# Attention transposes of two tiles packed four to a PSUM bank, output sums copied whole and moved by DMA, two sums inverted at once, another order of steps

## The chip, the cores and the metric

The kernel runs on one core of a Trainium2 chip. The metric is the device time of one execution in microseconds (us). A profile shows one execution: its span from the first to the last instruction, and the work of the engines TensorE (PE, with its weight loads as PEld), VectorE (DVE), ScalarE (ACT), GpSimd (POOL) and SyncE (SP, which here only issues DMAs).

## The reference, cut to what matters

```python
def _attn_ref(q, k, v, proj):            # q, k, v: 2 x 8 x 768 x 64; proj: 64 x 6
    q_bits = (np.einsum('bhsd,dk->bhsk', q, proj) > 0).astype(np.int64)
    k_bits = (np.einsum('bhsd,dk->bhsk', k, proj) > 0).astype(np.int64)
    q_bucket, k_bucket = np.sum(q_bits * powers, -1), np.sum(k_bits * powers, -1)
    mask = q_bucket[:, :, :, None] == k_bucket[:, :, None, :]
    scores = np.where(mask, scale * np.matmul(q, k.transpose(0, 1, 3, 2)), -1000000000.0)
    attn = np.exp(scores - np.max(scores, axis=-1, keepdims=True))
    attn = attn / (np.sum(attn, axis=-1, keepdims=True) + 1e-09)
    return np.matmul(attn, v)

def reference(**kwargs):
    x = _attn_ref(...)                   # -> 1536 tokens x 512
    x = _moe_ref(x, ...)                 # 8 experts, all on every token, weights from 8 rounds of row/column scaling
    return _moe2_ref(x, ...)             # 8 experts, each on 192 tokens, assigned greedily by logit
```

## The kernel before, in words

The program has three stages: attention (the first 267 us of the trace), the first mixture of experts and the second. The change touches attention alone.

Attention works in 8 **passes** of two heads each (`n` = 0 to 7). A pass has 12 **tiles** of 128 queries, six of each head; `t` counts tiles over all passes, `r` = 0 to 11 within a pass. Two neighbouring tiles make a **unit** (`unit`, line 267), whose output is 256 queries by 64 columns. Matmuls use float32r, a number split into a high and a low part where it needs more digits. A tile goes through these functions:

- `qk` (line 273): scores into one of two PSUM tiles `S0`, `S1`; four matmuls, the bucket mask is part of the operands.
- `soft` (282): the negated row maximum, on DVE. `expo` (287): exp and row sum, on ACT, into `e`. `inv` (293): 1/(sum + 1e-9), two DVE instructions on one column. `norm` (298): `e` times it, on POOL, into another tile `a`.
- `tr` (304): six 128x128 transposes of `a` on PE, three into each of two PSUM tiles `tp` (three buffers, which the preparation below also uses). `trh` (314): the high part, copied by ACT to `ah`. `trl` (318): the low part, on DVE to `al`.
- `av` (324): V times the transposed tiles of a unit, 12 matmuls of 256 columns into one half of the PSUM tile `O`, six in each of two steps. The stationary operand holds the high part of V beside the low part, so the two halves of `O`'s 128 partitions must still be added.
- `xa` (334): two ACT copies of 64 partitions by 256 columns carry them to `xm` and `xc`, one of them to other partitions. `xp` (348), on POOL and for the second head only: add the two, split the sum into high and low part for the next stage (`X`).

Beside that, `ahead` (362) prepares the next pass in its tiles r = 0 to 9: transposes of q and k (r = 0 to 3), bucket bits (4, 5), mask rows (6 to 9). `stack` (157) then moves q, k and mask rows into the operand tiles by DMA, six DMAs of 192 KB each after r = 1 and after r = 3, two after r = 7 and r = 9. `ahead_v` (367) prepares V on POOL and, in r = 11, issues the loads of q, k and v of the pass after next.

The order of all engines' instructions in attention is written out by hand: a loop over steps `t` (line 399) calls the functions in the order of `PLAN` or one of `PLANS` (lines 26 to 40), each with a lag, so that ('tr0', 3) in step t works on tile t - 3. Each engine runs its instructions in that order. SP issues its DMAs in that order too, and the weights of the next stage (`wgr`, line 462, and `raw`, line 432) stand behind the last of them in its queue.

Of the kernel before, what the change touches and what calls it, by code (L numbers as in the profile page):

```python
# [24 lines left out]

PLAN = (('norm', 2), ('qk', 0), ('soft', 0), ('tr0', 3), ('av', 5), ('expo', 1), ('pp', 0), ('th0', 3), ('inv', 1),
        ('tr1', 3), ('xa', 5), ('pa', 0), ('tl0', 3), ('pv', 0), ('pd', 0), ('th1', 3), ('tl1', 3), ('xp', 6))
PLANS = {
# [11 lines left out]
}  # L40
PREP_V = (3, 3, 6, 9)
# [14 lines left out]
def kernel(ctx, tc, q, k, v, proj, wg1, w1, w2, wg2, w1b, w2b, out):  # L56
# [225 lines left out]
    def soft(t):  # L282
        w = ap.tile([128, 4], F32, name="w", bufs=6)
        nc.vector.tensor_reduce(w[:, 0:1], Sp[t % 2], op=OP.max, axis=AX.X, negate=True)  # L284
        EN[t] = w

    def expo(t):
        w = EN[t]
        e = ap.tile([128, S], F32, name="e", bufs=2)
        nc.scalar.activation(e, Sp[t % 2], AF.Exp, bias=w[:, 0:1], scale=1.0, accum_out=w[:, 1:2])  # L290
        EN[t] = (e, w)

    def inv(t):
        e, w = EN[t]
        nc.vector.tensor_scalar(w[:, 2:3], w[:, 1:2], 1e-9, None, op0=OP.add)
        nc.vector.reciprocal(w[:, 3:4], w[:, 2:3])  # L296

    def norm(t):
        e, w = EN[t]
        a = ap.tile([128, S], F32, name="a", bufs=3)  # L300
        nc.gpsimd.tensor_tensor(a, e, w[:, 3:4].to_broadcast([128, S]), op=OP.mult)  # L301
        EN[t] = a

    def tr(t, c):
        u, i = divmod(t, 2)
# [6 lines left out]
        TP[t, c] = p[:, :384].rearrange("p (a b) -> p a b", a=3)  # L312

    def trh(t, c):
        u, i = divmod(t, 2)
        nc.scalar.activation(AT[u][0][:, 3 * c:3 * c + 3, i, :], TP[t, c], AF.Copy)  # L316

    def trl(t, c):
        u, i = divmod(t, 2)
        ah, al = AT[u]  # L320
        nc.vector.tensor_tensor(al[:, 3 * c:3 * c + 3, i, :], TP[t, c], rd(ah[:, 3 * c:3 * c + 3, i, :]), op=OP.subtract)  # L321


    def av(t):
        u, c = divmod(t, 2)
        n, s, j = unit(u)
        o = Op[:, u % 2]
        ah, al = AT[u]
        for kt in range(3 * c, 3 * c + 3):
            for a in (ah, al):  # L330
                nc.tensor.matmul(o, VS[n][:, kt, s].rearrange("p a d -> p (a d)"), a[:, kt].rearrange("p a b -> p (a b)"),  # L331
                                 start=(kt == 0 and a is ah), stop=(kt == R - 1 and a is al))

    def xa(t):
        u, c = divmod(t, 2)
        if c == 0:
            return
# [29 lines left out]
    def ahead_v(t):  # L367
# [829 lines left out]
```

## Time and profile before

| | |
|---|---|
| median of three runs | 1591.05 us (1590.64 to 1592.92) |
| the profiled execution | 1590.74 us, span 1589.0 us |
| PE busy over the span | 1557.7 us (98%) |
| DVE, ACT, POOL busy over the span | 812.7 us (51%), 471.3 us (30%), 269.0 us (17%) |
| busy from 14 to 268 us (254 us of attention): PE, DVE, ACT, POOL | 242.90, 221.51, 224.17, 214.01 us |
| granted TensorE clock there | 0.99 of full speed |

A matmul's recorded duration holds its fill and drain and overlaps the next one, so "busy" of PE says little. The distance from one matmul's start to the next one's start is what it really takes of the engine's time. The table's last two lines show a stage in which four engines are all above 84% busy, which the shares over the whole span hide.

### The profile page before, as it was taken

How to read it: one execution, taken by the hardware profiler on the slowest of the kernel's cores; microseconds unless marked ns; L12 is line 12 of the kernel's file. 1: busy time of each engine (PE TensorE's matmuls, PEld its weight loads, DVE VectorE, ACT ScalarE, POOL GpSimd, SP SyncE). 2: the span in 40 equal slices, each digit the busy share in tenths (PEclk: the TensorE clock that was granted, in tenths of full speed). 3: DMA queues.
4: the chain of work that ended last, by engine and by line, in shares of the span. 5: the costliest groups of instructions: out<-in, count | busy, mean ns of one | idle time of the engine just before them, and what ended most of it. 6: DMA issues, size and time to landing. Idle time of an engine off the chain costs nothing.

```text
span 1589.0 us, 21566 instructions
## 1 busy us (share of the span) xinstructions
PE 1557.7 (98%) x8482; PEld 1307.7 (82%) x8482; DVE 812.7 (51%) x1974; ACT 471.3 (30%) x950; POOL 269.0 (17%) x309
## 2 busy tenths in 40 slices
PE   8999998999999999999999999999999999899998
PEld 6888887788888888888888888888887767888998
DVE  6998888623433324333333332134677377667533
ACT  6998997212211210221221121021121210011343
POOL 4888886020000000000000000000000000111221
PEclk9999999999999999999999999999999999999999
DMA  8665561021200210110120020011000105555531
GB/s 189 150 146 134 124 157 37 31 93 37 70 1 14 71 35 14 53 54 1 40 80 0 14 80 27 1 53 53 1 14 14 41 31 196 174 189 188 191 137 31
DMA packets 81782, 117.75 MB, mean 74 GB/s; under 512 B 42960, under 2 KB 44496, under 8 KB 81680
## 3 DMA queue, kind: packets, MB, share of 16 engines
q1 hardware_dynamic: 75920, 105.15, 22.5%
q0 software_dynamic: 2144, 6.49, 1.3%
q10 hardware_dynamic: 3616, 4.72, 0.8%
q8 instruction: 67, 1.10, 0.3%
q14 instruction: 35, 0.29, 0.1%
HBM read 84.10 MB, written 7.86 MB: 58 GB/s over the span
## 4 chain that ended last, share of the span: by engine, by line
PE 89%; DVE 3%; ACT 3%; DMA 2%; POOL 1%; issue 1%; SPq 1%; ACTq 0%; POOLq 0%; DVEq 0%
PE hp L563 33%; PE yp L582 29%; PE hp L931 5%; PE yp L878 4%; PE tp L311 3%; PE O L331 3%; PE yp L983 3%; PE S L280 3%; PE yp L986 2%; PE sp L1065 1%; PE tp L202 1%; ACT e L290 1%; PE yp L988 1%; ACT ah L316 1%; DVE w L284 1%
## 5 line engine op out<-in xcount | busy, mean ns | idle before, releaser
L563 PE MATMUL hp<-X,big 128*128 128x512 f32 x2304 | 534.2, 392 | 0.0
L563 PEld LDWEIGHTS hp<-X,big 128*128 128x128 f32 x2304 | 431.9, 188 | 94.8
L582 PE MATMUL yp<-big 128*128 128x512 f32 x2016 | 462.2, 390 | 0.0
L582 PEld LDWEIGHTS yp<-big 128*128 128x128 f32 x2016 | 378.2, 188 | 79.5
L564 ACT ACTIVATE big<-hp 128x512 fp32r<-128x512 f32 x176 | 105.3, 598 | 763.0 <-PE hp L563 762.7
L565 DVE SCALAR_TENSOR_TENSOR big<-hp,big 128x512 fp32r<-128x512 f32 x176 | 121.6, 691 | 257.1 <-ACT big L564 257.0
L587 DVE SCALAR_TENSOR_TENSOR acc<-yp,P,acc 128x512 f32<-128x512 f32 x72 | 54.1, 751 | 259.3 <-PE yp L582 259.3
L859 POOL DMA_INDIRECT raw<-x2h,who x2 | 2.1, 1066 | 945.1 <-DVE wg2b L1050 944.8
L301 POOL TENSOR_TENSOR a<-e,w 128x768 f32<-128x768 f32 x96 | 140.7, 1468 | 45.4 <-DVE w L296 26.4
L321 DVE TENSOR_TENSOR al<-tp,ah 128x384 fp32r<-128x384 f32 x192 | 102.8, 547 | 18.9 <-ACT ah L316 18.5
L311 PE MATMUL tp<-ident,a 128*128 128x128 f32 x576 | 94.4, 276 | 8.7 <-ACT hot L233 2.9
L931 PE MATMUL hp<-raw,big 128*128 128x192 f32 x496 | 94.7, 337 | 2.1 <-ACT raw L910 2.1
L316 ACT ACTIVATE ah<-tp 128x384 fp32r<-128x384 f32 x192 | 90.9, 487 | 16.2 <-PE tp L311 15.7
L284 DVE TENSOR_REDUCE w<-S 128x1 f32<-128x768 f32 x96 | 91.1, 949 | 4.8 <-PE S L280 4.8
L311 PEld LDWEIGHTS tp<-ident,a 128*128 128x128 f32 x576 | 67.1, 140 | 25.1 <-issue 5.8
L290 ACT ACTIVATE e<-S,w 128x768 f32<-128x768 f32 x96 | 86.5, 901 | 0.7 <-POOL a L301 0.6
L428 DVE TENSOR_TENSOR big<-raw,big 128x1024 fp32r<-128x1024 f32 x63 | 76.6, 1221 | 14.1 <-ACT big L427 10.7
L931 PEld LDWEIGHTS hp<-raw,big 128*128 128x128 f32 x496 | 80.7, 192 | 3.6 <-ACT raw L910 2.4
L331 PE MATMUL O<-ah,vv 128*128 128x256 f32 x288 | 80.6, 309 | 0.5 <-ACT xm L346 0.5
L427 ACT ACTIVATE big<-raw 128x1024 fp32r<-128x1024 f32 x63 | 64.6, 1053 | 28.0 <-DMA raw<-in_moe_w_dram 25.0
L331 PE MATMUL O<-al,vv 128*128 128x256 f32 x288 | 72.8, 282 | 0.0
L538 DVE SCALAR_TENSOR_TENSOR junk<-acc,wg2b 128x512 bf16<-128x512 f32 x96 | 66.0, 688 | 1.9
(254 smaller groups left out, 1592.3 us busy)
## 6 DMA issues: line engine op xcount, KB each, us to landing
raw<-in_moe_w_dram SPq DMA_DIRECT2D x67, 512.0 KB, 3.3
big<-in_moe_w_dram SPq DMA_DIRECT2D x32, 1024.0 KB, 8.4
qa<-qhi SPq DMA_DIRECT2D x32, 192.0 KB, 3.8
qb<-qlo SPq DMA_DIRECT2D x16, 192.0 KB, 4.5
ka<-khi SPq DMA_DIRECT2D x16, 192.0 KB, 3.6
ka<-klo SPq DMA_DIRECT2D x16, 192.0 KB, 4.0
kb<-khi SPq DMA_DIRECT2D x16, 192.0 KB, 3.6
rv<-in_v_dram SPq DMA_DIRECT2D x16, 192.0 KB, 4.3
```

Of the source, the lines that this page charges most:

```text
L284: nc.vector.tensor_reduce(w[:, 0:1], Sp[t % 2], op=OP.max, axis=AX.X, negate=True)
L290: nc.scalar.activation(e, Sp[t % 2], AF.Exp, bias=w[:, 0:1], scale=1.0, accum_out=w[:, 1:2])
L301: nc.gpsimd.tensor_tensor(a, e, w[:, 3:4].to_broadcast([128, S]), op=OP.mult)
L311: nc.tensor.transpose(p[:, x * 128:x * 128 + 128], EN[t][:, (3 * c + x) * 128:(3 * c + x) * 128 + 128], ident)
L316: nc.scalar.activation(AT[u][0][:, 3 * c:3 * c + 3, i, :], TP[t, c], AF.Copy)
L321: nc.vector.tensor_tensor(al[:, 3 * c:3 * c + 3, i, :], TP[t, c], rd(ah[:, 3 * c:3 * c + 3, i, :]), op=OP.subtract)
L331: nc.tensor.matmul(o, VS[n][:, kt, s].rearrange("p a d -> p (a d)"), a[:, kt].rearrange("p a b -> p (a b)"), start=(kt == 0 and a is ah), ...
L563: nc.tensor.matmul(t, a, b, start=(i == 0), stop=(i == len(prods) - 1))
L564: nc.scalar.activation(hh[:, f], t, AF.Relu)
L565: nc.vector.scalar_tensor_tensor(hl[:, f], t, 0.0, rd(hh[:, f]), op0=OP.max, op1=OP.subtract)
L582: nc.tensor.matmul(t, a, b, start=(i == 0), stop=(i == len(prods) - 1))
L931: nc.tensor.matmul(opened[f], w[:, d, f * 128:f * 128 + 128], xt[:, d], start=(d == 0), stop=(d == HP - 1))
```

## The change

Four things change. **Transposes:** the twelve transposes of a unit's two tiles go into three PSUM places of four each (a place is one whole bank of 512 columns) instead of four places of three; `trh` and `trl` then handle 512 columns at a time, three times in a unit. The second place holds two blocks of the one tile and two of the other, so `ah` and `al` are laid out tile by tile, and `av` reads two stretches of 128 columns for its 256. **Sums:** V's high part now always stands first, so `xa` copies all 128 partitions of the unit's half of `O` in one ACT instruction; what has to change partitions is moved by DMA, one for the first head, two for the second head (from a tile `x1` with one buffer). **Inversion:** `inv` handles the sums of a unit's two tiles at once. **Order:** one plan of two steps (an even and an odd one) instead of five plans; `norm` writes in place, `e` has five buffers, and the lags grow: norm 3, transposes 4 to 6, av 7 and 8, `xa` 8, `xp` 10.

```diff
-PLAN = (('norm', 2), ('qk', 0), ('soft', 0), ('tr0', 3), ('av', 5), ('expo', 1), ('pp', 0), ('th0', 3), ('inv', 1),
...
+PLANS = ((('tr', 6, 2), ('norm', 3), ('qk', 0), ('av', 8, 1), ('tr', 4, 0), ('pv', 0), ('soft', 0), ('expo', 1), ('th', 6, 2),
...
     def inv(t):
         e, w = EN[t]
-        nc.vector.tensor_scalar(w[:, 2:3], w[:, 1:2], 1e-9, None, op0=OP.add)
-        nc.vector.reciprocal(w[:, 3:4], w[:, 2:3])
+        nc.vector.tensor_scalar(w[:, 4:6], w[:, 2:4], 1e-9, None, op0=OP.add)
+        nc.vector.reciprocal(w[:, 6:8], w[:, 4:6])
...
-        nc.gpsimd.tensor_tensor(a, e, w[:, 3:4].to_broadcast([128, S]), op=OP.mult)
+        nc.gpsimd.tensor_tensor(e, e, w[:, i:i + 1].to_broadcast([128, S]), op=OP.mult)
...
-        for x in range(3):
-            nc.tensor.transpose(p[:, x * 128:x * 128 + 128], EN[t][:, (3 * c + x) * 128:(3 * c + x) * 128 + 128], ident)
+        for y in range(4):
+            i, kt = divmod(4 * x + y, R)
+            nc.tensor.transpose(p[:, y * 128:y * 128 + 128], EN[t + i][:, kt * 128:kt * 128 + 128], ident)
...
-        nc.scalar.activation(AT[u][0][:, 3 * c:3 * c + 3, i, :], TP[t, c], AF.Copy)
+        ah = AT[t // 2][0].rearrange("p i a b -> p (i a b)")[:, 512 * x:512 * x + 512]
+        nc.scalar.activation(ah, TP[t, x], AF.Copy)
...
-                nc.tensor.matmul(o, VS[n][:, kt, s].rearrange("p a d -> p (a d)"), a[:, kt].rearrange("p a b -> p (a b)"),
+                nc.tensor.matmul(o, VS[n][:, kt, s].rearrange("p a d -> p (a d)"), a[:, :, kt],
...
     def xa(t):
...
-        nc.scalar.activation(xc[m0:m0 + 64, cs], o[c0:c0 + 64], AF.Copy)
-        nc.scalar.activation(xm[m0:m0 + 64, cs], o[m0:m0 + 64], AF.Copy)
+        if s == 0:
+            xm, xc = XP[n, j] = (ap.tile([128, 256], F32, name="xm", bufs=4), ap.tile([128, 256], F32, name="xc", bufs=4))
+            nc.scalar.activation(xm, o, AF.Copy)
+            nc.sync.dma_start(xc[:D], xm[D:])
+        else:
+            xm, xc = XP[n, j]
+            x1 = ap.tile([128, 256], F32, name="x1", bufs=1)
+            nc.scalar.activation(x1, o, AF.Copy)
+            nc.sync.dma_start(xm[D:], x1[:D])
+            nc.sync.dma_start(xc[D:], x1[D:])
...
-        if r % 2 == 0 and r >= 4 and n + 1 < NP:
-            prep_v(n + 1, r // 2 - 2)
+        if r in (8, 10) and n + 1 < NP:
+            prep_v(n + 1, r // 2 - 4)
+        if r in (0, 2) and 0 < n < NP:
+            prep_v(n, r // 2 + 2)
```

How the instructions stand now is shown at three places. The lines in rows of the changed kernel are those of its own file, some 12 to 15 lower.

On SP, from the mask rows of one pass (`kb<-hot`) over the loads (`rq`, `rk`, `rv`) to the next pass's q stack (`qa`, `qb`), before:

```order
L163 DMA kb_122<-hot_981 64x768 x2
L94 DMA rq<-in_q_dram 128x6x64 x2
L94 DMA rk<-in_k_dram 128x6x64 x2
L94 DMA rv<-in_v_dram 128x6x64 x2
L163 DMA qa_115<-qhi 64x768 x2
L163 DMA qb_117<-qlo 64x768
L163 DMA qa_115<-qhi 64x768 x2
L163 DMA qb_117<-qlo 64x768
```

and the same place in the changed kernel:

```order
L151 DMA kb_122<-hot_896 64x768 x2
L331 DMA xc<-xm 64x256
L82 DMA rq<-in_q_dram 128x6x64 x2
L82 DMA rk<-in_k_dram 128x6x64 x2
L82 DMA rv<-in_v_dram 128x6x64 x2
L331 DMA xc<-xm 64x256
L151 DMA qa_115<-qhi 64x768 x2
L151 DMA qb_117<-qlo 64x768
L151 DMA qa_115<-qhi 64x768 x2
L151 DMA qb_117<-qlo 64x768
L336 DMA xm<-x_1102 64x256
L337 DMA xc<-x_1102 64x256
```

A DMA of a finished sum (`xc<-xm`) has come between the mask rows and the loads, and the two DMAs that empty `x1` stand behind the six of the q stack.

On SP at the end of attention, from the last mask rows (`kb_118`) to the gate weights (`wgr`) and expert weights (`raw`) of the next stage, before:

```order
L163 DMA kb_118<-hot_3401 64x768 x2
L462 DMA wgr<-in_moe_w_gate_dram 128x4x8
L432 DMA raw<-in_moe_w_dram 128x1024 x4
L437 DMA raw<-in_moe_w_dram 128x2x512 x4
```

and in the changed kernel, from the last pass's sums on:

```order
L331 DMA xc<-xm 64x256 x3
L336 DMA xm<-x_3639 64x256
L337 DMA xc<-x_3639 64x256
L336 DMA xm<-x_3676 64x256
L337 DMA xc<-x_3676 64x256
L336 DMA xm<-x_3695 64x256
L337 DMA xc<-x_3695 64x256
L447 DMA wgr<-in_moe_w_gate_dram 128x4x8
L417 DMA raw<-in_moe_w_dram 128x1024 x4
L422 DMA raw<-in_moe_w_dram 128x2x512 x4
```

The weights of the next stage now stand behind the DMAs of the very last sum.

On PE, one step in the middle of attention, before (one tile's transposes in two groups of three, scores, one half of a unit's V product):

```order
L311 MATMUL tp<-ident,a 128x128 x3
L280 MATMUL S0_123<-ka0_120,qa0_119 128x512 [waits Activation_49]
L280 MATMUL S0_123<-ka0_120,qa0_119 128x256
L280 MATMUL S0_123<-kb0_122,qb0_121 128x512
L280 MATMUL S0_123<-kb0_122,qb0_121 128x256
L311 MATMUL tp<-ident,a 128x128 x3
```

and in the changed kernel the end of an odd step, with the first two groups of the even step behind it:

```order
L298 MATMUL tp<-ident,e 128x128 x8
L268 MATMUL S_123<-ka_120,qa_119 128x512
L268 MATMUL S_123<-ka_120,qa_119 128x256
L268 MATMUL S_123<-kb_122,qb_121 128x512
L268 MATMUL S_123<-kb_122,qb_121 128x256
L320 MATMUL O<-ah,vv 128x256
```

An even step has two groups of four transposes and an odd step one; the eight in the first row are the odd step's group and the even step's first. The number of transposes, scores and V products of two steps is the same as before.

## Rows read from the trace of the kernel before

**Rows 1.** Busy time by stretch: start:end, length; each engine busy (instructions); clock, DMA share, GB/s

```profile
80.00:112.00 32.00, 31.18 (x227) 27.96 (x224) 28.66 (x71) 29.21 (x71) 27.66 (x28) 1.00 0.63 136
```

**Rows 2.** PE in order of time, first bit matmul of passes 0 and 6: start, us

```profile
25.12 0.45 PE L202 MATMUL tp<-qhi,pjh 128*128 128x384 f32 x1
...
213.13 0.34 PE L202 MATMUL tp<-qhi,pjh 128*128 128x384 f32 x1
```

**Rows 3.** PE in order of time, one step in the middle of attention

```profile
60.44 0.49 PE L311 MATMUL tp<-ident,a 128*128 128x128 f32 x3
60.68 0.60 PE L280 MATMUL S<-ka,qa 128*128 128x512 f32 x2
...
61.47 0.49 PE L311 MATMUL tp<-ident,a 128*128 128x128 f32 x3
...
62.51 0.34 PE L225 MATMUL tp<-bits,pat 128*128 128x384 f32 x1
```

**Rows 4.** Chain of waits in order of time, one piece: start, us, what

```profile
56.42 1.05 PE tp L202 x6
```

**Rows 5.** Costliest groups of the page: line, engine, tiles, count | busy, mean ns | idle before

```profile
L564 ACT ACTIVATE big<-hp 128x512 fp32r<-128x512 f32 x176 | 105.3, 598 | 763.0 <-PE hp L563 762.7
L565 DVE SCALAR_TENSOR_TENSOR big<-hp,big 128x512 fp32r<-128x512 f32 x176 | 121.6, 691 | 257.1 <-ACT big L564 257.0
...
L321 DVE TENSOR_TENSOR al<-tp,ah 128x384 fp32r<-128x384 f32 x192 | 102.8, 547 | 18.9 <-ACT ah L316 18.5
...
L316 ACT ACTIVATE ah<-tp 128x384 fp32r<-128x384 f32 x192 | 90.9, 487 | 16.2 <-PE tp L311 15.7
```

**Rows 6.** Groups of ACT from 14 to 268 us, same columns

```profile
L345 ACT ACTIVATE xc<-O 64x256 f32<-64x256 f32 x48 | 18.2, 378 | 5.3 <-PE O L331 3.9
```

**Rows 7.** Groups of POOL from 14 to 268 us, same columns

```profile
L301 POOL TENSOR_TENSOR a<-e,w 128x768 f32<-128x768 f32 x96 | 140.7, 1468 | 45.4 <-DVE w L296 26.4 <-ACT hot L233 12.9 <-ACT xm L346 2.4
...
L358 POOL TENSOR_TENSOR xm<-xm,xc 128x256 f32<-128x256 f32 x23 | 16.9, 734 | 0.2 <-ACT xm L346 0.2
...
L359 POOL TENSOR_TENSOR X<-xm,zero 128x256 fp32r<-128x256 f32 x23 | 14.1, 613 | 1.8
```

**Rows 8.** SP in order of time: last mask rows of a pass, then a load

```profile
71.19 1.11 SPq L163 DMA_DIRECT2D kb<-hot  x2
72.35 1.34 SPq L94 DMA_DIRECT2D rq<-in_q_dram  x2
```

**Rows 9.** SP in order of time: first and last DMAs of one q stack

```profile
111.61 1.16 SPq L163 DMA_DIRECT2D qa<-qhi  x2
...
115.65 0.56 SPq L163 DMA_DIRECT2D qb<-qlo  x1
```

**Rows 10.** PE in order of time, first q transposes of a pass and what they waited for

```profile
140.21 0.52 PE L173 MATMUL tp<-ident,rq 128*128 128x128 f32 x3 [0.93 <-DMA rq<-in_q_dram]
```

**Rows 11.** Tile `rq`: from DMA issue to landing

```profile
DMA to landing us min/median/max: 2.3/3.4/4.5
```

**Rows 12.** DMA issues from 226 to 250 us: tiles, count, KB each, median us to landing

```profile
raw<-in_moe_w_dram SPq DMA_DIRECT2D x3, 512.0 KB, 4.5
kb<-hot SPq DMA_DIRECT2D x2, 192.0 KB, 2.8
wgr<-in_moe_w_gate_dram SPq DMA_DIRECT2D x1, 16.0 KB, 2.6
```

**Rows 13.** PE in order of time, from the last units into the next stage

```profile
265.34 0.38 PE L331 MATMUL O<-ah,vv 128*128 128x256 f32 x1 [0.53 <-ACT xm L346]
...
267.14 0.40 PE L476 MATMUL sp<-X,wgs 128*16 128x512 f32 x1
...
276.81 2.35 PE L563 MATMUL hp<-X,big 128*128 128x512 f32 x9
```

**Rows 14.** ACT in order of time: first three weight conversions of the next stage

```profile
268.13 2.96 ACT L427 ACTIVATE big<-raw 128x1024 fp32r<-128x1024 f32 x3
```

**Rows 15.** DVE in order of time: first weight conversion and what it waited for

```profile
270.47 1.22 DVE L428 TENSOR_TENSOR big<-raw,big 128x1024 fp32r<-128x1024 f32 x1 [3.41 <-POOL X L360]
```

More of the change, by code (lines that the diff above doesn't have):

```diff
@@ L282, in soft @@
     def soft(t):
-        w = ap.tile([128, 4], F32, name="w", bufs=6)
-        nc.vector.tensor_reduce(w[:, 0:1], Sp[t % 2], op=OP.max, axis=AX.X, negate=True)
-        EN[t] = w
+        if t % 2 == 0:
+            EN[t] = EN[t + 1] = ap.tile([128, 8], F32, name="w", bufs=5)
+        nc.vector.tensor_reduce(EN[t][:, t % 2:t % 2 + 1], Sp[t % 2], op=OP.max, axis=AX.X, negate=True)
     def expo(t):
-        w = EN[t]
-        e = ap.tile([128, S], F32, name="e", bufs=2)
-        nc.scalar.activation(e, Sp[t % 2], AF.Exp, bias=w[:, 0:1], scale=1.0, accum_out=w[:, 1:2])
+        w, i = EN[t], t % 2
+        e = ap.tile([128, S], F32, name="e", bufs=5)
+        nc.scalar.activation(e, Sp[i], AF.Exp, bias=w[:, i:i + 1], scale=1.0, accum_out=w[:, 2 + i:3 + i])
         EN[t] = (e, w)
@@ L314, in trh @@
-    def trh(t, c):
-        u, i = divmod(t, 2)
-        nc.scalar.activation(AT[u][0][:, 3 * c:3 * c + 3, i, :], TP[t, c], AF.Copy)
[L318 to L325, printed above, removed]
+        i = 6 + t % 2
+        nc.gpsimd.tensor_tensor(e, e, w[:, i:i + 1].to_broadcast([128, S]), op=OP.mult)
+        EN[t] = e
@@ new lines, in tr, with trh @@
+    def tr(t, x):
+        p = aps.tile([128, 512], F32, name="tp", bufs=3)
+        for y in range(4):
+            i, kt = divmod(4 * x + y, R)
+            nc.tensor.transpose(p[:, y * 128:y * 128 + 128], EN[t + i][:, kt * 128:kt * 128 + 128], ident)
+        TP[t, x] = p
+    def trh(t, x):
+        if x == 0:
+            AT[t // 2] = (ap.tile([128, 2, R, 128], F32R, name="ah", bufs=2),
+                          ap.tile([128, 2, R, 128], F32R, name="al", bufs=2))
+        ah = AT[t // 2][0].rearrange("p i a b -> p (i a b)")[:, 512 * x:512 * x + 512]
+        nc.scalar.activation(ah, TP[t, x], AF.Copy)
@@ L326, in av, with trl @@
+    def trl(t, x):
+        ah, al = (y.rearrange("p i a b -> p (i a b)")[:, 512 * x:512 * x + 512] for y in AT[t // 2])
+        nc.vector.tensor_tensor(al, TP[t, x], rd(ah), op=OP.subtract)
+    def av(t, c):
+        u = t // 2
         n, s, j = unit(u)
-        o = Op[:, u % 2]
+        o = Op[:, u % 2].rearrange("p (i b) -> p i b", i=2)
         ah, al = AT[u]
@@ L330, in av @@
             for a in (ah, al):
-                nc.tensor.matmul(o, VS[n][:, kt, s].rearrange("p a d -> p (a d)"), a[:, kt].rearrange("p a b -> p (a b)"),
+                nc.tensor.matmul(o, VS[n][:, kt, s].rearrange("p a d -> p (a d)"), a[:, :, kt],
                                  start=(kt == 0 and a is ah), stop=(kt == R - 1 and a is al))
     def xa(t):
-        u, c = divmod(t, 2)
-        if c == 0:
-            return
+        u = t // 2
         n, s, j = unit(u)
-        if s == 0 and j == 0:
-            XP[n] = (ap.tile([128, S], F32, name="xm", bufs=1), ap.tile([128, S], F32, name="xc", bufs=1))
-        xm, xc = XP[n]
         o = Op[:, u % 2]
-        m0, c0 = 64 * s, 64 - 64 * s
-        cs = slice(j * 256, j * 256 + 256)
-        nc.scalar.activation(xc[m0:m0 + 64, cs], o[c0:c0 + 64], AF.Copy)
-        nc.scalar.activation(xm[m0:m0 + 64, cs], o[m0:m0 + 64], AF.Copy)
+        if s == 0:
[8 more added lines that the diff above has]
+            nc.sync.dma_start(xc[D:], x1[D:])
     def xp(t):
-        u, c = divmod(t, 2)
-        n, s, j = unit(u)
-        if c == 0 or s == 0:
+        n, s, j = unit(t // 2)
+        if s == 0:
             return
         b, hp = divmod(n, HP)
-        xm, xc = XP[n]
-        cs = slice(j * 256, j * 256 + 256)
+        xm, xc = XP[n, j]
         g, o2 = divmod(b * S + j * 256, 512)
         xh, xl = X[g][:, hp, 0, o2:o2 + 256], X[g][:, hp, 1, o2:o2 + 256]
-        nc.gpsimd.tensor_tensor(xm[:, cs], xm[:, cs], xc[:, cs], op=OP.add)
-        nc.gpsimd.tensor_tensor(xh, xm[:, cs], zero.to_broadcast([128, 256]), op=OP.add)
-        nc.gpsimd.tensor_tensor(xl, xm[:, cs], rd(xh), op=OP.subtract)
+        nc.gpsimd.tensor_tensor(xm, xm, xc, op=OP.add)
+        nc.gpsimd.tensor_tensor(xh, xm, zero.to_broadcast([128, 256]), op=OP.add)
+        nc.gpsimd.tensor_tensor(xl, xm, rd(xh), op=OP.subtract)
     def ahead(t, part):
@@ L371, in ahead_v @@
                 prep_v(0, i)
-        if r % 2 == 0 and r >= 4 and n + 1 < NP:
-            prep_v(n + 1, r // 2 - 2)
+        if r in (8, 10) and n + 1 < NP:
+            prep_v(n + 1, r // 2 - 4)
+        if r in (0, 2) and 0 < n < NP:
+            prep_v(n, r // 2 + 2)
         if r == TU - 1 and n + 2 < NP:
             load(n + 2)
-    STEPS = dict(qk=qk, soft=soft, expo=expo, inv=inv, norm=norm, tr0=lambda t: tr(t, 0), tr1=lambda t: tr(t, 1),
-                 th0=lambda t: trh(t, 0), th1=lambda t: trh(t, 1), tl0=lambda t: trl(t, 0), tl1=lambda t: trl(t, 1),
-                 av=av, xa=xa, xp=xp, pp=lambda t: ahead(t, 0), pa=lambda t: ahead(t, 1), pd=lambda t: ahead(t, 2),
+    STEPS = dict(qk=qk, soft=soft, expo=expo, inv=inv, norm=norm, tr=tr, th=trh, tl=trl, av=av, xa=xa, xp=xp, pp=lambda t: ahead(t, 0), pa=lambda t: ahead(t, 1), pd=lambda t: ahead(t, 2),
                  pv=ahead_v)
@@ L398 @@
     load(1, "v")
-    for t in range(NT + max(lag for _, lag in PLAN)):
-        for nm, lag in plan(t):
+    for t in range(NT + max(x[1] for x in PLANS[0])):
+        for nm, lag, *part in PLANS[t % 2]:
             if 0 <= t - lag < NT:
-                STEPS[nm](t - lag)
+                STEPS[nm](t - lag, *part)
     order.close()
```

23 lines of the change are left out of this document (6 added, 17 removed), and 11 rows, old and new, of the table PLANS.

## The prediction

> **What bounds the kernel now.** I read the busy times by stretch first, then PE in order of time inside attention, then the groups of ACT, DVE and POOL, and last the queue of SP. In 32 us of attention ACT is busy 29.2, DVE 28.7, POOL 27.7 [rows 1]: no engine has room, though all but PE look idle over the whole span. PE is paced by its work plus waits. From the first bit matmul of pass 0 to that of pass 6 it takes 188.0 us [rows 2], six passes of 31.34. The reader is to measure the work by distances between starts. A step runs from 60.44 to 62.51, so a tile costs 2.07: two groups of three transposes at 0.24, scores 0.79, the rest (1.04 less 0.24) 0.80 for half a unit's V product [rows 3]. Twelve tiles are 24.8. Preparation adds twelve bit matmuls, 1.05 for six [rows 4], four mask matmuls of the same shape (0.18 each), and four groups of transposes, in all 3.8. So 28.6 of 31.34 is work and **2.7 us per pass is waiting**. After attention PE is the bound to the end, so a microsecond won or lost before or at the border stays.
>
> **Part by part.** All sums are made against the profiled execution's 1590.74 (span 1589.0 and 1.74 around it), 0.3 below the median of 1591.05.
>
> *Transposes and copies.* PE's work stays: 24 groups of three become 18 of four, 72 transposes of 0.08 either way. ACT's copies per unit go from four of 487 ns to three of 512 columns; the nearest row of that shape is 598 [rows 5], so 1948 becomes 1794. Two sum copies of 378 [rows 6] become one of the same columns: 378 less. Together 0.53 us per unit, 3.2 per pass. DVE's low parts go from four of 547 to three of about 691 [rows 5], 0.12 less, and one inversion instead of two saves a further pair of small instructions. None of this is on the path by itself. It buys back the part of the 2.7 that is PE waiting for a place that ACT or DVE still holds.
>
> *The strided operand.* `av` now reads two stretches of 128 columns. No row shows such a read. From below it costs nothing; from above, every matmul would cost what the first of a group shows, some 0.08 more over 576 matmuls, 46 us. Stretches of 512 bytes are close to contiguous, so I take 0.
>
> *In-place norm and the larger lags.* The in-place addition takes 734 and the addition of the same size into another tile 613 [rows 7]; I take the same 1468 for the norm. Two steps more of lag empty the start and fill the end by the same work; I take 0 for both ends of attention (-1.5 to +1.5).
>
> *The load is later.* Before, the load of the pass after next follows the mask rows of r = 9 on SP without a wait [rows 8]. Now a DMA of r = 10's sum stands between, and it waits for the sum. From the end of that unit's V product: 0.2 until the copy starts (estimate), 0.38 copy [rows 6], 0.55 issue, 0.67 for the first `rq` [rows 8], 3.4 until the second lands [rows 11], and 0.4 for what ACT has queued before the copy (estimate). That is 5.6. PE meanwhile has a transpose group (0.32), an odd step (0.79 + 0.80 + 0.32) and an even one (2.22), in all 4.45, then needs `rq`. It waits 1.15 per pass; all transposes, scores and V products stand behind it. That such a late load stops PE is seen once before, 0.93 [rows 10]. Bounds by the landing's ends, 2.3 and 4.5: 0.05 to 2.25.
>
> *One buffer of x1.* The two DMAs of r = 2's sum stand behind the q stack, which holds SP for 4.6 us [rows 9] from about 0.6 into that step (estimate: q's high part is the last thing that ACT does in the step before). So they leave by 5.75 and land 2.8 later, as the mask rows do in a quiet queue [rows 12]: 8.5. The next copy into `x1` is wanted two steps on, at 6.7. ACT waits 1.8, and its copies and the exp behind it wait too. PE needs `O`'s bank, and it does wait for that copy [rows 13]; it has 2.16 of other work, less 0.6 for the copy. About 0.3 reaches PE at r = 4, 0.1 at r = 6 behind the k stack: 0.4. Bounds: 0 and 1.5 if the landing takes a microsecond more. POOL's addition waits for the same landing with the norms queued behind it; the transposes that it makes late come in r = 10, just ahead of the load wait, and of these two only the longer counts.
>
> With 0.6 left for everything else (a fifth of the old waits, my choice; 0.2 to 1.5) a pass waits 1.15 + 0.4 + 0.6 = 2.15 instead of 2.7. Six passes: **-3.3**.
>
> *The border to the next stage.* Here the queue alone decides. Before, gate and expert weights were fetched at least 17 us ahead (by 250 at the latest) [rows 12]; PE went from the last V product straight into the gate matmuls at 267.14 and ran steadily on expert matmuls from 276.81, 9.7 later [rows 13]. Now these loads stand behind the last sum's DMAs. After the last V product: 0.6 copy, 1.1 two issues, then `wgr`, which lands 2.6 after its issue, so gate matmuls begin 4.3 late. The weights: 0.6 further on SP, 4.5 landing (6.8), ACT 0.99 [rows 14], DVE 1.22 [rows 15] (9.0), and only then is a buffer free for the fourth block, which an expert's first group needs: 3.8 for a load that has the queue for itself (between 2.6 and 4.5), ACT 0.99. PE is steady at 13.8 instead of 9.7: **+4.1** (2 to 5.5). In the old run the last POOL sum was what DVE's first conversion waited for [rows 15]; now the loads are late anyway.
>
> Sum: 1590.74 - 3.3 + 4.1 = 1591.5, and 1591.8 as a median: call it **1592, no change that can be told**.
>
> **Rivals.**
>
> *B, the transfers are hidden: 1582.* If a landing takes 2.3 as the shortest `rq` does [rows 11], the load wait is 0.05 and `x1`'s is hidden by PE's other work. A pass waits 0.65, 2.05 less than before: 12.3 for six, less 4.1 at the border. For it: SP has pauses in every pass. Against: the median is 3.4, and the loads' bytes are in 256-byte pieces. The Trainium skill, DMA: Bandwidth & Descriptors (Anatomy of one DMA), gives about 2.0 us plus the bytes at 436 GB/s, for a DMA issued by GpSimd; by that a load of 192 KB would land after 2.45 (an estimate), its wait be 0.2, and the time about 1583. The trace says 2.8 for the same size in a quiet queue [rows 12], so the rule is too short here.
>
> *C, the small DMAs queue behind the stack's bytes: 1598.* The DMA engines move 136 GB/s at a share of 0.63 [rows 1], so 216 at full share. Six times 192 KB then need 5.5 us, 0.9 more than SP needs to issue them, and the two DMAs of `x1` land that much later. ACT's wait becomes 2.7, the part of it that reaches PE grows by 0.9, and POOL, which holds the norms behind the same landing, cannot make it good: it has two norms and an addition of three, 2.94 + 2.1 [rows 7], per unit, against 4.8 of PE. Six passes: +5.4 to +7. It decides from a landing of about 3.5. For it: the stack's DMAs do land slowly; against: a pass has four quieter units to catch up. The Trainium skill, the same page (Queues, rings and completion order), says that each engine takes descriptors in ring order, which is this mechanism; no row here isolates it.
>
> *D, the waits before are not ACT's or DVE's: 1604.* Then the 2.7 stay, the new 1.55 come on top: +9.3 and +4.1. Against it: 29 of 32 us busy on both [rows 1] leaves little other cause.
>
> **How the numbers follow.** My forecast 0.40 (own range 1588 to 1595), B 0.25, C 0.27, D 0.08. About 0.2%, 3.2 us, is what a measurement of this kernel can tell from no change, so "same" is 1587.9 to 1594.2. Of the forecast 0.30 lies there, 0.06 above, 0.04 below; of B 0.21 below, 0.04 inside; of C 0.23 above, 0.04 inside; D above. Faster 0.25, same 0.38, slower 0.37. The range that leaves two in ten out runs from B's edge to C's: 1583 to 1600.
>
> **What would show it.** In the new profile: passes of 30.5 to 31.2 between first bit matmuls; PE waiting for `rq` at the first preparation of a pass; ACT's `x1` copies waiting 1 to 3 us for DMAs at r = 4; ACT and DVE busy share down by about a tenth; `wgr` issued after the last `x1` DMA, the first gate matmul more than 4 us behind the last V product. The forecast is wrong if passes come under 30 (B) or over 32 (C, D), or if the first gate matmul follows at once.

## The result and the profile after

The changed kernel takes **1606.35 us** (median of 4 runs, 1604.27 to 1608.25) against 1591.99 for the kernel before in the same session: ratio 1.0091, 95% interval 1.0076 to 1.0106. The forecast was 1592, no change, with 1583 to 1600 as its range. It was wrong: the kernel is 14.4 us slower.

The profiled execution took 1606.66 (span 1605.0), 15.9 more than the one before. First the groups that answer to [rows 5 to 7], from ACT, DVE and POOL inside attention (count | busy, mean ns | idle before, and what ended it):

```profile
L306 ACT ACTIVATE ah<-tp 128x512 fp32r<-128x512 f32 x144 | 86.9, 605 | 21.1 <-PE tp L298 19.4
L335 ACT ACTIVATE x<-O 128x256 f32<-128x256 f32 x24 | 9.3, 388 | 25.0 <-DMA xc<-x 22.7 <-PE S L268 1.7 <-PE O L320 0.4
...
L310 DVE TENSOR_TENSOR al<-tp,ah 128x512 fp32r<-128x512 f32 x144 | 98.2, 683 | 26.1 <-ACT ah L306 23.8
...
L290 POOL TENSOR_TENSOR e<-e,w 128x768 f32<-128x768 f32 x96 | 139.1, 1470 | 32.6 <-DVE w L285 25.3 <-ACT khi L168 6.1 <-PE S L268 0.8
L347 POOL TENSOR_TENSOR xm<-xm,xc 128x256 f32<-128x256 f32 x24 | 17.6, 731 | 25.7 <-DMA xc<-x 17.5 <-DMA xm<-x 8.3
```

Every duration is as forecast: 605 for the copy (598 was taken), 683 for the low part (691), 1470 for the norm in place (1468). The loss is in the last column: the copy into `x1` waits 22.7 us for DMAs, and POOL's sum, which had waited for nothing [rows 7], waits 25.7.

The same stretch as in [rows 1], by busy time, and the first bit matmuls of passes 0 and 6, as in [rows 2]:

```profile
80.00:112.00 32.00, 30.02 (x218) 27.36 (x217) 28.26 (x49) 25.68 (x57) 26.90 (x25) 1.00 0.68 155
```

```profile
26.17 0.67 PE L190 MATMUL tp<-qhi,pjh 128*128 128x384 f32 x1
...
218.36 0.42 PE L190 MATMUL tp<-qhi,pjh 128*128 128x384 f32 x1
```

ACT has lost 3.5 us of work in 32 (29.21 to 25.68; about a tenth was forecast), and still six passes take 192.2 instead of 188.0. The border, in order of time: PE's last V matmul, first gate matmul and first long row of expert matmuls, then SP's last issues, then DVE's first instruction on the gate weights:

```profile
275.81 0.28 PE L320 MATMUL O<-al,vv 128*128 128x256 f32 x1
281.19 0.61 PE L461 MATMUL sp<-X,wgs 128*16 128x512 f32 x1 [5.10 <-DVE wgs L450]
...
290.49 2.36 PE L548 MATMUL hp<-X,big 128*128 128x512 f32 x9
```

```profile
277.42 0.46 SPq L336 DMA_DIRECT2D xm<-x  x1
277.93 0.59 SPq L337 DMA_DIRECT2D xc<-x  x1
278.56 0.59 SPq L447 DMA_DIRECT2D wgr<-in_moe_w_gate_dram  x1
279.20 6.54 SPq L417 DMA_DIRECT2D raw<-in_moe_w_dram  x4
```

```profile
280.63 0.27 DVE L449 CAST wgs<-wgr 128x32 fp32r<-128x32 f32 x1 [5.96 <-DMA wgr<-in_moe_w_gate_dram]
```

`wgr` leaves behind the last `x1` DMAs, as forecast, and the gate matmuls start 5.3 after the V product's end (275.93, its last start plus the 0.12 from one V matmul to the next), where before they followed at once [rows 13].

**Where the 16 us of span went**, by distances between such starts in both traces: first bit matmul of pass 0 +1.05; six passes +4.2; from pass 6 to the last V product +3.55 (57.57 against 54.02); from there to the first copy of hidden rows (ACT's first `big<-hp`) +4.9 (17.0 against 12.1); the expert stage -0.5; the part behind it, from the first copy of hidden rows into `X`, +2.8. The last is not the change's: that part is 364.1 to 367.1 us long in the traces below, whichever kernel. There PE idles for 4 us of one stretch of 20 while POOL and DVE work, and the granted clock of that stretch was 0.91 before and 0.80 after. PE's work in and right behind it, from `sp<-ident,raw` to `yp<-acc,big`, took 14.0 us before and 16.8 after, which is all of the 2.8:

```profile
1364.80:1384.80 20.00, 16.00 (x132) 13.93 (x130) 11.33 (x52) 2.63 (x7) 4.30 (x5) 0.91 0.46 149
```

```profile
1377.90:1397.90 20.00, 15.91 (x114) 13.76 (x113) 10.57 (x48) 1.98 (x5) 4.30 (x5) 0.80 0.47 151
```

### The profile page after: what moved, and what is told of

Same layout as the page of the kernel before. It is cut to its first block, busy times and chain, and to the rows that moved or that the text cites. A ratio compares the mean times of both kernels' runs of the same rounds, so it can differ in the third digit from the quotient of the medians.

```text
span 1605.0 us, 21405 instructions
## 1 busy us (share of the span) xinstructions
PE 1560.2 (97%) x8482; PEld 1314.0 (82%) x8482; DVE 815.7 (51%) x1830; ACT 452.0 (28%) x854; POOL 268.5 (17%) x309
## 4 chain that ended last, share of the span: by engine, by line
PE 83%; DMA 4%; DVE 4%; POOL 4%; issue 2%; SPq 1%; ACT 1%; POOLq 0%; ACTq 0%
PE hp L548 32%; PE yp L567 29%; PE hp L916 5%; PE yp L863 4%; PE yp L968 3%; POOL e L290 2%; PE O L320 2%; PE yp L971 2%; PE tp L298 2%; PE sp L1050 1%; PE S L268 1%; DMA xm<-x 1%; DMA xc<-x 1%; SPq L151 1%; DMA raw<-in_moe_w_dram 1%
## 5 line engine op out<-in xcount | busy, mean ns | idle before, releaser
L290 POOL TENSOR_TENSOR e<-e,w 128x768 f32<-128x768 f32 x96 | 139.1, 1470 | 32.6 <-DVE w L285 25.3
L310 DVE TENSOR_TENSOR al<-tp,ah 128x512 fp32r<-128x512 f32 x144 | 98.2, 683 | 26.1 <-ACT ah L306 23.8
L306 ACT ACTIVATE ah<-tp 128x512 fp32r<-128x512 f32 x144 | 86.9, 605 | 21.1 <-PE tp L298 19.4
L298 PE MATMUL tp<-ident,e 128*128 128x128 f32 x576 | 85.4, 275 | 6.8 <-POOL e L290 5.9
L320 PE MATMUL O<-ah,vv 128*128 128x256 f32 x288 | 74.3, 287 | 7.8 <-ACT x L335 6.8
L298 PEld LDWEIGHTS tp<-ident,e 128*128 128x128 f32 x576 | 66.3, 141 | 10.8 <-POOL e L290 7.8
L320 PEld LDWEIGHTS O<-ah,vv 128*128 128x128 f32 x288 | 54.4, 189 | 15.6 <-ACT x L335 10.9
```

The costliest lines, as they stand in the source:

```text
L290: nc.gpsimd.tensor_tensor(e, e, w[:, i:i + 1].to_broadcast([128, S]), op=OP.mult)
L298: nc.tensor.transpose(p[:, y * 128:y * 128 + 128], EN[t + i][:, kt * 128:kt * 128 + 128], ident)
L306: nc.scalar.activation(ah, TP[t, x], AF.Copy)
L310: nc.vector.tensor_tensor(al, TP[t, x], rd(ah), op=OP.subtract)
```

## The experiments

Each was timed beside the kernel before. "Pass" is the mean of the five from pass 1's first bit matmul to pass 6's, "border" the time from the last V product to the first copy of hidden rows, both from one trace; the ratio is to the kernel before.

| kernel | median us | ratio (95%) | pass | border |
|---|---|---|---|---|
| before | 1592.0 to 1593.1 | 1 | 31.37 | 12.1 |
| changed | 1606.35 | 1.0091 (1.0076 to 1.0106) | 32.49 | 17.0 |
| e1 three `x1` | 1603.9 | 1.0069 (1.0055 to 1.0083) | 32.78 | 17.2 |
| e2 sums at lag 14 | 1610.5 | 1.0105 (1.0090 to 1.0119) | 33.18 | 17.8 |
| e3 DMAs by ACT | 1614.8 | 1.0148 (1.0129 to 1.0168) | 33.51 | 19.2 |
| e4 no DMA, two ACT copies | 1589.1 | 0.9978 (0.9970 to 0.9987) | 30.67 | 12.1 |
| e5 three `x1`, lag 12 | 1595.7 | 1.0014 (1.0005 to 1.0023) | 30.86 | 17.1 |
| e6 last pass's DMAs by ACT | 1610.4 | 1.0105 (1.0091 to 1.0120) | 33.30 | 21.6 |
| e7 e5 + e6 + load earlier | 1596.2 | 1.0022 (1.0013 to 1.0031) | 30.85 | 18.1 |
| e8 e4 + idle DMAs | 1598.5 | 1.0037 (1.0024 to 1.0050) | 31.21 | 16.6 |
| e9 e5 + V's parts spread | 1592.2 | 0.9998 (0.9989 to 1.0007) | 30.97 | 16.4 |
| e10 e5 + end by ACT copies | 1589.7 | 0.9984 (0.9975 to 0.9993) | 30.84 | 12.1 |
| e11 e9 + e10 | 1589.0 | 0.9979 (0.9970 to 0.9988) | 30.56 | 12.1 |
| e12 e4 + V's parts spread | 1593.2 | 1.0005 (0.9996 to 1.0014) | 30.54 | 12.1 |
| e13 e9 + load earlier | 1587.3 | 0.9964 (0.9952 to 0.9976) | 29.58 | 17.0 |
| e14 e11 + load earlier | 1583.6 | 0.9943 (0.9930 to 0.9956) | 29.69 | 12.1 |

### One landing, two engines: e1, e2, e5

The changed kernel at one place, in order of time: SP's last DMA of a k stack and the two of a sum, then ACT, POOL and PE:

```profile
156.97 0.77 SPq L151 DMA_DIRECT2D kb<-khi  x1
157.84 1.44 SPq L336 DMA_DIRECT2D xm<-x  x1
159.32 0.60 SPq L337 DMA_DIRECT2D xc<-x  x1
```

```profile
161.94 0.38 ACT L335 ACTIVATE x<-O 128x256 f32<-128x256 f32 x1 [2.36 <-DMA xc<-x]
```

```profile
161.96 0.73 POOL L347 TENSOR_TENSOR xm<-xm,xc 128x256 f32<-128x256 f32 x1 [1.74 <-DMA xm<-x]
```

```profile
162.38 0.39 PE L320 MATMUL O<-ah,vv 128*128 128x256 f32 x1 [1.14 <-ACT x L335]
```

The sum's DMAs stand behind the stack, and when they land they release ACT and POOL within 0.02 us of each other: ACT may write `x1` again, POOL may add. Which one stops PE? e1 frees the first, e2 the second.

```diff
-            x1 = ap.tile([128, 256], F32, name="x1", bufs=1)
+            x1 = ap.tile([128, 256], F32, name="x1", bufs=3)   # e1, e5; xm, xc bufs=3
-          ('xp', 10), ...
+          ('xp', 14), ...                                      # e2; e5: 12
```

> The changed kernel with three buffers of x1 instead of one (xm and xc three instead of four, to make room). Theory T1, the single buffer: ACT's copies into x1 wait 20 us in all for the DMAs that read the copy before, and hold the exps, the copies of the transposes and O's bank behind them. Then passes fall from 32.0 to about 30.5 and the time by 9 to 13, to 1594 to 1597. Theory T2, the landing: POOL's sums wait 24 us for the DMAs' landings with the norms queued behind them, whatever x1 has. Then ACT's waits go, POOL's stay, and the time stays within 4 of 1606.

> The changed kernel with POOL's sums four steps later (lag 14 instead of 10); one buffer of x1 as before. T2 (POOL held by the landings): its 24 us of waits go, passes fall to 30.5 to 31, the time to about 1596. T1 (the single buffer of x1): ACT's 20 us of waits stay and the time stays within 4 of 1606.

> The changed kernel with three buffers of x1 (xm and xc three instead of four) and POOL's sums two steps later (lag 12): both ends of the landing are given time at once. Theory T3: one late landing held two engines side by side, ACT through x1 and POOL through the sum, and either alone stops PE (alone the first gave 2 us, the second nothing). Then both waits go and passes fall from 32.0 to 30.4, as with the sums moved by ACT (30.4); 1606 less 7 x 1.6 less 1 at the end: 1593 to 1596. Rival T4: the queue and the bytes of the DMAs slow the passes in another way too; passes stay over 31.3 and the time over 1600.

PE's largest waits from 50 to 250 us (us in all, times, longest), first in the changed kernel, then e1, e2 and e5:

```profile
PE O L320 <- ACT x L335: 6.3, 10, 1.7
PE tp L298 <- POOL e L290: 4.5, 6, 0.8
PE tp L161 <- DMA rq<-in_q_dram: 1.3, 3, 0.8
PE tp L298 <- DVE al L310: 0.5, 3, 0.2
```

```profile
PE tp L298 <- POOL e L290: 13.4, 12, 2.8
```

```profile
PE tp L298 <- POOL e L290: 7.6, 12, 1.5
PE O L320 <- ACT x L335: 7.2, 7, 2.1
```

```profile
PE tp L298 <- POOL e L290: 9.9, 6, 1.7
```

With three `x1` PE no longer waits for `O`; it waits for the norms behind POOL's sum instead, and only 2.4 us are won (the passes of its one trace are no shorter). With the sums later POOL's sum waits for nothing, PE waits for `O` as before, and the time does not fall: 1610.5, just above T1's range. Both at once win 10.7, as T3 said (1593 to 1596), and passes come to 30.86 (30.4 was expected). In the same 200 us POOL's sums still wait 19.0 for landings in e1, ACT's copies 18.5 in e2, and in e5 neither waits. One landing held two engines, and each hid the other. For POOL's side alone e2 is not a clean test: a lag of 14 puts the sums into the steps r = 8, 10 and 0, in which POOL prepares V too.

### Is it the queue, the bytes or the wait: e3, e4, e8

e3 issues the same DMAs on ACT. e4 undoes them: two ACT copies per unit and V's parts laid out as before, the rest of the change kept. e8 is e4 with the nine DMAs of a pass issued at the same places on SP, out of `xc` into tiles that nobody reads.

```diff
-            xm, xc = XP[n, j]; x1 = ...; nc.scalar.activation(x1, o, AF.Copy); nc.sync.dma_start(...) x2
+        nc.scalar.activation(xc[m0:m0 + 64], o[c0:c0 + 64], AF.Copy)      # e4, e8
+        nc.scalar.activation(xm[m0:m0 + 64], o[m0:m0 + 64], AF.Copy)
+            nc.sync.dma_start(DX[k % 3][...], xc[m0:m0 + 64])             # e8
-            nc.sync.dma_start(xm[D:], x1[:D])
+            nc.scalar.dma_start(xm[D:], x1[:D])                           # e3, all three
```

> The changed kernel with all DMAs of the sums issued by ACT, right behind its copy, instead of SP. They no longer stand behind the q and k stacks, and the next pass's load and the next stage's weights no longer stand behind them. Price: three issues of about 0.5 per two units on ACT, 4.5 per pass, with ACT busy 25.5 of 32. If the order in SP's queue is the loss (my forecast's mechanism, at the border and in the passes): passes 30 to 31 and PE 5 earlier at the border, 1590 to 1596. If the DMA engines' bytes are the loss (the landing is late whichever queue issues it): border -5, passes as they are, 1601. If ACT's issues cost as much as its waits: over 1603.

> The changed kernel with the sums moved as before (two ACT copies of 64 partitions per unit, V's parts laid out as before, no DMA); the packing of the transposes, one inversion for two, the norm in place and the new order stay. If the DMAs are the whole loss: no wait for x1 or landings, load and weights leave SP at once, border as before the change, ACT busy 2.3 per pass more; 1582 to 1589, faster than before. If the packing or the order (lags, late release of places) loses too: 1592 or more.

> The kernel with the sums moved by ACT (1589), and beside them the same nine DMAs per pass from SP, at the same places in its queue, with the same bytes, into tiles that nothing reads. No engine waits for a landing; what they cost is the queue's order and the bytes alone. If the waits for landings are the loss in the passes (T3): passes 30.4 to 30.8 (the load is late again, 1 us at most), border +4.9, so 1594 to 1597. If queue and bytes are the loss (T4): passes near 32, 1603 to 1606.

e4 takes 1589.1, 3.5 less than the kernel before: packing, one inversion for two, the norm in place and the new order are worth that, and moving the sums by DMA instead of by ACT costs 17 us (1606.35 less 1589.1). PE's waits in e4, from 50 to 250 us, hold none for a norm:

```profile
PE O L320 <- ACT xm L333: 2.2, 9, 0.3
PE tp L161 <- DMA rq<-in_q_dram: 1.1, 1, 1.1
```

e8 lies between its two cases (1598.5). Nobody waits for a landing in it: 9.4 come back, 4.5 of them at the border and 0.54 per pass. So queue and bytes are a smaller part in the passes; the waits on landings are the larger (e8's passes 31.2, the changed kernel's 32.5). e3 is its third case and worse, 1614.8; PE's longest wait in it, 8.0 us from 50 to 250, is for DVE's `al`, which follows ACT's copies. ACT in order of time there, around one sum, and the landings of `xc`, first issued by SP (the changed kernel), then by ACT:

```profile
158.07 0.38 ACT L335 ACTIVATE x<-O 128x256 f32<-128x256 f32 x1
158.49 0.47 ACTq L336 DMA_DIRECT2D xm<-x  x1
158.98 1.09 ACTq L337 DMA_DIRECT2D xc<-x  x1
160.12 0.60 ACT L306 ACTIVATE ah<-tp 128x512 fp32r<-128x512 f32 x1 [1.66 <-PE S L268]
```

```profile
DMA to landing us min/median/max: 1.9/2.1/4.6
```

```profile
DMA to landing us min/median/max: 1.9/3.2/5.0
```

The two issues hold ACT for 0.47 and 1.09 us between a copy and the next one that PE needs. The two medians mix places. In the changed kernel the two DMAs of one sum landed so, first right behind a q stack (at 151.5), then with no stack in flight (at 162.4):

```profile
DMA to landing us min/median/max: 2.5/2.9/3.2
```

```profile
DMA to landing us min/median/max: 1.9/2.0/2.0
```

Over the passes, as far as the trace tells landings, `xm<-x` behind a stack took 3.2 to 3.3 and `xc<-x` 2.5 to 2.6 (medians), without one 1.9 and 2.0. Issued by ACT past the stack, in e3, they took 3.7 to 3.8 and 4.4.

### The border: e6, e7, e10

```diff
-            nc.sync.dma_start(xm[D:], x1[:D])
+            (nc.scalar if n == NP - 1 else nc.sync).dma_start(xm[D:], x1[:D])   # e6, e7: all three
-        if r == TU - 1 and n + 2 < NP:
+        if r == TU - 2 and n + 2 < NP:                                          # e7
+        if n == NP - 1: ...two nc.scalar.activation as in e4, V laid out alike  # e10
```

> The changed kernel with the DMAs of the sums of the last pass alone issued by ACT, so that in SP's queue nothing of the attention's end stands before the next stage's weights. If the border costs what the traces say (last V product to first copy of hidden rows 17.0 instead of 12.1): 4.5 to 5 less, 1601 to 1602, the first gate matmul right behind the last V product, passes as they are. If the weights are late for another reason (their places in memory come free late): within 2 of 1606.

> The two before together (three x1, sums at lag 12, last pass's DMAs by ACT), and the load of the pass after next one step earlier, ahead of the sum's DMA in SP's queue. If T3 holds and the border is the rest: passes 30.2 to 30.5, border as before the change, 1587 to 1590, level with the sums moved by ACT (1589). If T4 holds: over 1596.

> The kernel with three x1 and sums at lag 12 (1595.7), the sums of the last pass alone moved by ACT (two copies per unit, V's parts of that pass laid out as before). The two runs with the last DMAs on ACT's queue put the weights' loads ahead and gained nothing: DVE's first conversion then waited 8.4 us for POOL's last sum, that is for the landing. Theory B1: the border costs what the copy, the landing and POOL's sum behind it take, whichever queue. Then without a landing at the end the border is as before the change (last V product to first copy of hidden rows 12.1 instead of 17.1) and the time 1590 to 1592. Rival B2: the weights' places come free late for another reason (lags): border stays over 15, time 1594 to 1597.

With the last DMAs on ACT's queue the gate weights come early and the gate matmuls follow the V product at once, but the border is longer, 21.6 and 18.1, and neither run reached a time that it was given for a cause (1610.4 and 1596.2). DVE's first weight conversion in e7, then in e10:

```profile
273.56 1.23 DVE L414 TENSOR_TENSOR big<-raw,big 128x1024 fp32r<-128x1024 f32 x1 [8.45 <-POOL X L350]
```

```profile
268.06 1.23 DVE L421 TENSOR_TENSOR big<-raw,big 128x1024 fp32r<-128x1024 f32 x1 [4.06 <-POOL X L357]
```

It waits for POOL's last sum, which waits for the last landing. The border was late for two reasons side by side, SP's order and this wait; either alone is enough (e8 has only the first: 16.6; e7 only the second: 18.1). e10 has neither, and its border is that of the kernel before. e6 had the changed kernel's order in all passes but the last, yet its passes are 33.30 against 32.49, each in one trace; that spread stays open.

### What was left in the passes: e9, e11 to e14

In e5 all of PE's waits are for a norm, 1.65 per pass. POOL there, in order of time (rows left out are further parts of the same sums):

```profile
156.93 0.83 POOL L245 TENSOR_TENSOR vv<-rv,zero 128x384 fp32r<-128x384 f32 x1
157.72 0.75 POOL L347 TENSOR_TENSOR xm<-xm,xc 128x256 f32<-128x256 f32 x1
...
159.93 2.90 POOL L290 TENSOR_TENSOR e<-e,w 128x768 f32<-128x768 f32 x2
162.78 1.04 POOL L248 TENSOR_TENSOR vv<-rv,vv 128x384 fp32r<-128x384 f32 x1
163.78 0.73 POOL L347 TENSOR_TENSOR xm<-xm,xc 128x256 f32<-128x256 f32 x1
...
165.97 2.90 POOL L290 TENSOR_TENSOR e<-e,w 128x768 f32<-128x768 f32 x2
```

It works without a pause, 19 us in all, and two of its three sums share a step with a part of V (r = 8 and 10). Before the change no step had both: sums at r = 1, 3, 5, V's parts at 4, 6, 8, 10. The change moved the sums to 4, 6, 8 and V's parts to 8, 10, 0, 2, which leaves one shared step; e5's own lag of 12 makes it two. e9 spreads V's parts so that none is shared, and PE's next wait shows (from 50 to 250 us, below the edit):

```diff
-        if r in (8, 10) and n + 1 < NP:
-            prep_v(n + 1, r // 2 - 4)
-        if r in (0, 2) and 0 < n < NP:
-            prep_v(n, r // 2 + 2)
+        if r in (0, 2, 4, 5) and 0 < n < NP:
+            prep_v(n, (0, 2, 4, 5).index(r))
```

```profile
PE tp L161 <- DMA rq<-in_q_dram: 3.3, 3, 1.8
PE tp L298 <- POOL e L290: 2.6, 7, 1.1
```

> The kernel with three x1 and sums at lag 12 (1595.7, passes 30.86), and V's four parts of a pass prepared by POOL at r = 0, 2, 4, 5 of the pass itself instead of r = 8, 10 of the one before and 0, 2. What is left of the waits there is one of 1.66 us per pass, PE for a norm at r = 11, with POOL busy without a pause for 19 us before it (three sums, two V parts, norms). Theory T5, POOL's order: that wait goes to under 0.5, passes 29.6 to 30, time 1587 to 1590. Rival T6: PE is then held by something else as long (ACT's or DVE's order, the starts of groups): passes stay over 30.5, time within 3 of 1595.7.

> Both edits before together (V's parts spread; last pass's sums by ACT). If T5 and B1 hold: passes 29.6 to 30, border 12.1, time 1581 to 1585, faster than the sums moved by ACT throughout (1589). If only one holds: 1587 to 1592.

> The kernel with all sums moved by ACT (1589, passes 30.4, POOL busy 28 of 32), with V's parts spread in the same way. If POOL's order is what is left there too: passes 29.6 to 30, time 1584 to 1586. If there ACT (busy 29.8 of 32) sets the pace: passes stay 30.2 to 30.5, within 2 of 1589.

> The kernel with three x1, sums at lag 12 and V's parts spread (1592.2), with the load of the pass after next one step earlier, ahead of the r = 10 sum's DMA in SP's queue. My forecast put 1.15 per pass on the later load; in the changed kernel PE waited 1.3 for rq in eight passes, in this one 3.3, 1.8 of it in one pass. If the load's lateness is what has come up behind POOL's wait: no wait for rq, passes without the 33 us one, 2 to 4 less, 1588 to 1590. If the wait for rq only trades with another: within 1.5 of 1592.

> The kernel with all of these and the last pass's sums by ACT (1589.0), with the load one step earlier too. PE waited 2.1 for rq there. If the load's lateness is what is left: 1586 to 1587.5, faster than any so far. If not: within 1.5 of 1589.

e9 won 3.5, between its two cases by time, T6's case by its passes (30.97): POOL's wait fell, and a wait for `rq` came up in its place. e11 gave little for the same reason, as much as was expected if one theory alone holds. e12 was a miss: the same edit is no gain where ACT moves the sums, where PE waited for no norm that could be won (e4's waits, above). Its median is 4 above e4's though its profiled execution was at 1588.8; the eight executions above 1592 had a granted clock of 0.992 to 0.994 over the span, the profiled one 0.996. Why is open. With the load ahead of the sum's DMA (the edit of e7, worth nothing in the passes there) e13 wins another 4.8, and e14 takes **1583.6**, 0.6% under the kernel before. PE's largest wait in e13 and the stretch of [rows 1] in e14:

```profile
PE tp L298 <- POOL e L290: 4.6, 9, 1.4
```

```profile
80.00:112.00 32.00, 31.75 (x242) 30.33 (x241) 29.96 (x52) 28.12 (x62) 29.44 (x28) 1.00 0.76 174
```

## Why the prediction was wrong

The forecast had six passes 3.3 shorter, by waits of 2.15 in a pass of 30.75; the five passes from pass 1 on took 32.49. The term that failed is "one buffer of x1".

**Work of a pass, 28.6.** Right. PE runs the same 220 matmuls in the same order in each of these passes, in the changed kernel and in e1 to e14. For each place in that order take the shortest distance from a start to the next in any of the traces: they add up to 28.56. What a pass shows above that is its waits, also those too short for the lists above. Each is put to the matmul that starts late (us per pass, mean of five passes of one trace, rounded):

| kernel | V products (`O`) | transposes of `e` | transposes of q and k | the rest | all |
|---|---|---|---|---|---|
| changed | 1.80 | 1.39 | 0.46 | 0.28 | 3.92 |
| e4 | 1.13 | 0.34 | 0.35 | 0.28 | 2.11 |
| e5 | 0.19 | 1.96 | 0.00 | 0.15 | 2.30 |
| e9 | 0.30 | 0.60 | 1.25 | 0.27 | 2.40 |
| e13 | 0.19 | 0.56 | 0.11 | 0.15 | 1.01 |

PE's busy time would have misled: 30.02 of 32 at a pass of 32.2 makes 30.2 in the changed kernel, and 31.73 at 29.5 makes 29.2 in e13, for the same work. Distances between starts don't have that fault.

**"One buffer of x1 ... 0.4."** This step failed, and with it the gain. The way was as told (two DMAs behind the stack, ACT and POOL behind their landing), and the landing came about as forecast: from the stack's first issue to the landing that frees `x1` it took 7.7 to 9.3 us, 8.2 in the mean, against 7.9. What the landing did to PE was mis-sized. ACT waited 1.7 to 3.3 at r = 4 (2.1 in the mean, 1.8 forecast) and 1.4 to 2.4 behind the k stack in four passes of six, and PE's other work hid much less of it: the V products cost 1.80 per pass, and 0.19 once `x1` and the sums have time (e5). Wrong was also the sentence that POOL's late norms fall where the load wait hides them: PE lost 1.39 at the transposes of `e`, while e4, with the same order on POOL and no landing, loses 0.34. By these differences the landing cost 1.6 + 1.05 = 2.65 per pass, against bounds of 0 and 1.5.

**"The load is later", 1.15.** The changed kernel loses 0.46 at the q and k transposes; PE came there late itself, after its waits for `O` and the norms. Uncovered, the lateness is there: 1.25 in e9, where moving the load (e13) leaves 0.11 and is worth 4.8 us. In e7, where PE waits for a norm, it changes nothing in the passes.

**"0.6 left for everything else."** In the changed kernel 3.92 - 2.65 - 0.46 = 0.8 is left, near the forecast; that is a difference between kernels and was not measured by itself. The 1.96 of e5 is no measure of it, since its own lag brought the second shared step, and spreading V's parts (e9) takes 1.36 of it away. ACT's and DVE's relief was real: from 50 to 250 us PE had waited 4.7 for them, in the kernel before:

```profile
PE tp L311 <- ACT hot L233: 2.7, 6, 0.5
PE tp L311 <- DVE al L321: 1.4, 6, 0.3
...
PE tp L173 <- DVE w L284: 0.6, 1, 0.6
```

In the changed kernel 0.5 is left. So a pass is 28.6 + 2.65 + 0.46 + 0.8 = 32.5, not 28.6 + 2.15.

**Both ends of attention, 0.** The first bit matmul of pass 0 was 1.05 later in this trace, but not by the change: e5 and e14 run the same instructions up to there and have it at 24.5 and 24.3, earlier than the kernel before. The end from pass 6 was 3.55 longer. About 1.8 of that is work that the longer lags move there, 12 V matmuls of 0.12 and 5 transposes of 0.08; the first of the six passes has 12 V matmuls less and took 29.76, so that the six passes' +4.2 looks better by 1.4 than it is. The rest of the 3.55 is waits that no run takes apart.

**The border, +4.1.** Right in size and order: the first gate matmul 5.3 late (4.3 forecast), steady expert matmuls 14.6 after the last V product (13.8), +4.9 in all. What I had called settled by the late loads, POOL's last sum, was a second reason close behind the first: in the changed kernel it ended 1.7 us before DVE's first weight conversion began, and with the loads early (e7) DVE waited for it.

**The free parts.** The strided operand costs nothing, as the V matmuls with `al` show, before and after (from one V matmul's start to the next it is 0.12 us in the median in both):

```profile
L331 PE MATMUL O<-al,vv 128*128 128x256 f32 x288 | 72.8, 282 | 0.0
```

```profile
L320 PE MATMUL O<-al,vv 128*128 128x256 f32 x288 | 72.9, 282 | 0.0
```

The norm in place costs what was forecast.

**The rivals.** C (1598) named the mechanism best: POOL cannot make a late landing good. Its reason, a landing 0.9 later than forecast, is not borne out (8.2 against 7.9 from the stack's first issue); the stack's bytes do slow the two DMAs, to 3.2 and 2.5 from 1.9 and 2.0, but the forecast's landing was long enough for that. D has the time, 1604, by another reason: the old waits for ACT and DVE went, and larger new ones came.

## What to carry to other kernels

A landing that two engines wait for must be given time on both sides (a further buffer for the writer, a longer lag for the reader); freeing one showed 2.4 us or none of the 10.7. When an edit moves work, list every instruction that shares its new step, on each engine, also the small ones with slack: POOL, busy 27.8 of 32 us in e5, was full for 19 in a row, since the sums' new lag met V's parts. An edit that gives nothing may be waiting behind another: the earlier load was worth nothing in e7 and 4.8 us in e13.

## What the runs showed of the hardware

In the changed kernel a 64x256 DMA between two tiles landed 1.9 to 2.3 us after its issue by SP where nothing else was in flight, and right behind a stack of six 192 KB DMAs after 3.2 to 3.3 (`xm<-x`) and 2.5 to 2.6 (`xc<-x`, medians). Issued by ACT past such a stack, in e3, the same two landed after 3.7 to 3.8 and 4.4 (medians), and an issue took 0.47 to 1.89 us of ACT's time. The Trainium skill, Trainium Kernel Development and Optimization (Key Constraints), says that DMAs of all issuing queues share the same engines and interleave, so that a second queue saves issue time alone; the longer landings past the stack agree. On ACT, which PE waits for, the issue time was not saved but moved.
